# Linear attention and routed experts on one core: fp32 products in halves of the array, and exponentials after the transposes

## The chip, the cores and the metric

The kernel runs on one core of one Trainium2 chip. The metric is the device time of one execution in microseconds (us), the median of three runs. TensorE multiplies matrices, VectorE and ScalarE work on elements and rows, GpSimd does both and issues indirect DMAs, SyncE issues DMAs. Every engine serves its own instructions in order.

## The reference

```python
def phi(x):                                   # x: (4, 8, 576, 64), scaled by 64 ** -0.25
    proj = np.einsum('bhsd,md->bhsm', x, omega)     # 128 features
    h = proj - np.sum(x * x, axis=-1, keepdims=True) / 2.0
    h = h - np.max(h, axis=-1, keepdims=True)
    return np.exp(h) / np.sqrt(m)
q_p, k_p = phi(q_s), phi(k_s)
kv, z = np.einsum('bhsm,bhsd->bhmd', k_p, v), np.sum(k_p, axis=2)
num = np.einsum('bhsm,bhmd->bhsd', q_p, kv)
den = np.einsum('bhsm,bhm->bhs', q_p, z)[..., None] + 1e-06
x = (num / den)                               # as 2304 tokens of 8 * 64 columns
expert_idx = np.argmax(x @ w_gate, axis=1)    # 8 experts
...
h = np.maximum(np.einsum('ecd,edf->ecf', disp, w1), 0.0)   # 512 -> 1024
y = np.einsum('ecf,efd->ecd', h, w2)                       # 1024 -> 512
out[i] = gate_w[i] * y[expert_idx[i], pos[i]]              # up to a capacity per expert
```

## The kernel before, in words

There are three stages, written in one order for every engine.

**Keys.** A pair of heads has nine tiles of 128 tokens; two pairs are handled side by side, one on partitions 0 to 63 and one on 64 to 127, and such a double pair is a chunk (4 batches, 2 chunks each, 72 steps). Keys come transposed, head dimension on partitions. A step projects one tile of both pairs to 256 columns (`project`, L120): the keys are split into two parts of 12 bits (`split`, L113; GpSimd, for the first chunk ScalarE and VectorE), and three products of 256 columns in the rounded 4-byte type add to fp32 accuracy (L122 to L124). `exponent` (L127) takes the maxima of both halves (VectorE, L129) and two exponentials of 128 columns with the maximum as bias (ScalarE, L132). Three steps later `kv_acc` (L188) sums exponentials against values in fp32 (L192: exponentials are the stationary side, 65 columns of values and ones move). After a chunk `kv_gate` (L201) multiplies its sums by the gate weights.

**Queries.** The loop over 18 token tiles has four steps each, one per head pair: projection and exponentials as for the keys, three steps later transposes by TensorE (L446) and a copy to SBUF (ScalarE, L448), six steps later the numerators (`numer`, L451; L462: 73 columns hold sums, denominator and gate logits). `normalise` (L473) divides on VectorE and stores the tile to DRAM. A tile that crosses from one batch to the next has its numerators in two parts of 64 tokens. `route` (L338) turns logits of five to seven tiles into slots and scatters them into a table (GpSimd, L92); `first_item` (L396) and `first_rows` (L427) read the first token's expert, load and split its weights, load a table's rows (L312), gather tokens (GpSimd, L317) and transpose them (`transpose_x`, L324). These are generators: the loop calls `steps` twice per step, and each call advances every one to its next `yield`; `pause(n)` waits n calls.

**Items.** An item is 576 slots of one expert; three run here, the others are skipped by a condition. `mm1` (L649) is the first product, 8 x 2 banks of 12 products (L656 to L658) with evictions on ScalarE and VectorE (L661 to L666); `mm2` and `mm2_rest` (L668, L680) are the second, the last 64 slots in two column halves side by side (L685, fp32). During an item weights and rows of the next are loaded, split (`HI_AT`, `LO_AT`; high parts on GpSimd, L108, low parts mostly on VectorE, L111) and transposed. The remaining routing runs in the first product of the first item (`il`, L717).

PSUM has eight banks of 512 columns: three for projections and first products, two for sums, numerators and second products, two for transposes, one for small things.

Of the kernel before, what the change touches and what calls it, by code (L numbers as in the profile page):

```python
# [24 lines left out]
SLOTS = 576              # slots of one expert item  # L25
FIRST_CUTS = [0, 128, 384, 768, 1152]  # the first keys come in parts
# [5 lines left out]
T0 = 5                   # token tiles that the first item looks at  # L32
QT = 3                   # most token tiles of a query chunk
# [7 lines left out]
HI_AT = ({0: ((1, 2), (1, 3), (2, 0), (2, 1), (2, 2), (2, 3))}, {0: ((2, 0),), 1: ((2, 1),), 3: ((2, 2),), 4: ((2, 3),)})  # L41
LO_AT = ({0: ((1, 2),), 1: ((1, 3),), 3: ((2, 0),), 4: ((2, 1),)}, {1: ((2, 0),), 2: ((2, 1),), 5: ((2, 2),), 6: ((2, 3),)})
# [8 lines left out]
def attention_moe(ctx, tc, kT, qT, va, om, wg, w1, w2, cap, ident, tri, desc, lst, tab0, out):  # L51
# [7 lines left out]
    ps = ctx.enter_context(tc.tile_pool(name="ps", bufs=2, space=PSUM))  # L59
# [4 lines left out]
    def bank(tag, name, bufs=2):  # L64
        return ps.tile([128, 512], F32, tag=tag, name=name, bufs=bufs)

    om_sb = const.tile([128, M], F32, name="om_sb")
    whi = const.tile([128, 2 * M], F32R, name="whi")
    wlo = const.tile([128, 2 * M], F32R, name="wlo")
# [4 lines left out]
    # counts of tokens: small whole numbers, exact in bfloat16  # L74
# [14 lines left out]
    # Slots are unique, so are the tokens behind them: scatters into one array  # L89
    # touch different rows and need no order among themselves.  # L90
# [13 lines left out]
    def split_hi(hi, raw, eng=None):  # L104
        if eng is nc.scalar:
            nc.scalar.copy(hi, raw)
        else:
            nc.gpsimd.tensor_scalar(hi, raw, 1.0, 1.0, op0=ALU.mult, op1=ALU.mult)  # L108

    def split_lo(lo, raw, hi, eng=None):  # L110
        (eng or nc.gpsimd).tensor_tensor(lo, raw, hi.bitcast(F32), op=ALU.subtract)  # L111

    def split(hi, lo, raw, ehi=None, elo=None):  # L113
        split_hi(hi, raw, ehi)
        split_lo(lo, raw, hi, elo)
# [4 lines left out]
    def project(hi, lo, nm, spare=False):  # L120
        pj = (bank("tr", f"pj{nm}") if spare else bank("pj", f"pj{nm}", 3))[:, 0 : 2 * M]
        nc.tensor.matmul(pj, hi, whi, start=True, stop=False)  # L122
        nc.tensor.matmul(pj, lo, whi, start=False, stop=False)  # L123
        nc.tensor.matmul(pj, hi, wlo, start=False, stop=True)  # L124
        return pj

    def exponent(pj, nm):  # L127
        mx = small.tile([128, 2], F32, tag="mx", name=f"mx{nm}", bufs=6)
        nc.vector.tensor_reduce(mx, pj.rearrange("p (a m) -> p a m", a=2), op=ALU.max, axis=AX.X, negate=True)  # L129
        ex = small.tile([128, 2 * M], F32, tag="ex", name=f"ex{nm}", bufs=6)  # L130
        for i in range(2):
            nc.scalar.activation(  # L132
                ex[:, i * M : (i + 1) * M], pj[:, i * M : (i + 1) * M], AF.Exp, bias=mx[:, i : i + 1], scale=1.0
            )
        return ex

# [5 lines left out]
    def load_q(c):  # L142
        n0, n1 = QB[c] * 128, QB[c + 1] * 128
        w = n1 - n0
        raw = qp.tile([128, NP, QT * 128], F32, tag="qraw", name=f"qraw{c}")
        nc.sync.dma_start(raw[:, :, 0:w], qT[:, :, n0:n1])
        qc[c] = raw, w

    def split_q(c, p):
        if p == 0:  # L150
            hi = qp.tile([128, NP, QT * 128], F32R, tag="qhi", name=f"qhi{c}")
            lo = qp.tile([128, NP, QT * 128], F32R, tag="qlo", name=f"qlo{c}")
            qc[c] = hi, lo, *qc[c]
        hi, lo, raw, w = qc[c]
        split(hi[:, p, 0:w], lo[:, p, 0:w], raw[:, p, 0:w])

# [4 lines left out]
    kp = kstack.enter_context(tc.tile_pool(name="kpool", bufs=2))  # L161
    chunks, first = {}, []

    def load_k(b, g):
        raw = kp.tile([128, W], F32, tag="kraw", name=f"kraw{b}{g}")
        hi = kp.tile([128, W], F32R, tag="khi", name=f"khi{b}{g}")
        lo = kp.tile([128, W], F32R, tag="klo", name=f"klo{b}{g}")
        v = kp.tile([128, 2, 10 * VW], F32, tag="v", name=f"v{b}{g}")
        src = va[b, :, 2 * g : 2 * g + 2, :]
        if b == 0 and g == 0:  # L170
            for i, (c0, c1) in enumerate(zip(FIRST_CUTS, FIRST_CUTS[1:])):
                nc.sync.dma_start(raw[:, c0:c1], kT[b, :, g * W + c0 : g * W + c1])
                if i == 2:
                    nc.sync.dma_start(v[:, :, 0 : 4 * VW], src[:, :, 0 : 4 * VW])
# [6 lines left out]
        chunks[b, g] = hi, lo, v, raw  # L181

    def split_k(b, g, c0, c1, ehi=None, elo=None):
        hi, lo, _, raw = chunks[b, g]
        split(hi[:, c0:c1], lo[:, c0:c1], raw[:, c0:c1], ehi, elo)

    # a pair's 9 token tiles: 4 of head A, one of both, 4 of head B
    def kv_acc(b, g, t, ex, acc):  # L188
        v = chunks[b, g][2]
        a, z, o = (t, t + 1, 0) if t < 4 else ((4, 6, 0) if t == 4 else (t + 1, t + 2, VW))  # L190
        for i in range(2):
            nc.tensor.matmul(  # L192
                acc[:, i * 2 * VW + o : i * 2 * VW + o + (z - a) * VW],
                ex[:, i * M : (i + 1) * M],
                v[:, i, a * VW : z * VW],
                start=(t == 0 and i == 0),
                stop=(t == 8),
                skip_group_check=True,
            )

    def kv_gate(b, g, acc):  # L201
        yield from pause(2)
        kv = kv_sb[b][:, 4 * g : 4 * g + 4, :]
        nc.vector.tensor_copy(kv[:, :, 0:VW], acc[:, 0 : 4 * VW].rearrange("p (h c) -> p h c", h=4))
        yield from pause(2 if (b, g) < (B - 1, 1) else 16)
        kvc = small.tile([128, 2 * M], F32, tag="kvc", name=f"kvc{b}{g}", bufs=1)
        nc.scalar.copy(kvc.rearrange("p (h c) -> p h c", h=4), kv[:, :, 0:D])
        yield from pause(4)
        tr = bank("tr", f"ktr{b}{g}")
# [5 lines left out]
        yield from pause(4)  # L215
        sm = bank("sm", f"ksm{b}{g}", 1)
        for i in range(2):
            nc.tensor.matmul(
                sm[:, i * 2 * E : (i + 1) * 2 * E],
                kvT[:, i * M : (i + 1) * M],  # L220
                wg_sb[:, 2 * g + i, :],
                start=True,
                stop=True,
            )
# [5 lines left out]
    # the tensor engine's clock rises with use: keep it busy until the first keys are there  # L230
# [594 lines left out]
```

## Time and profile before

| | us |
|---|---|
| median of 3 runs | 338.39 |
| lowest, highest | 337.31, 339.58 |
| span of the profiled execution | 336.1 |
| keys, until the last sums | 71.0 |
| queries | 85.1 |
| three items | 169.8 |
| after the last transposes | 10.1 |

The profiled execution has no other time than its span, from the first to the last instruction. The stages are read from the trace: the last key sums end at 71.0, the first product of the first item starts at 156.1.

### The profile page before, as it was taken

The page shows a single profiled execution, that of the slowest core. Times are in us where ns is not written, and L with a number is a line of the kernel's source. Part 1 is how long each engine was busy: PE and PEld are TensorE (multiplying, and loading weights), DVE is VectorE, ACT ScalarE, POOL GpSimd, SP SyncE. Part 2 cuts the span into 40 slices and gives each one's busy share as a digit, 9 for nine tenths or more (in the row PEclk, how much of TensorE's full clock was granted, in tenths as well). Part 3 has the DMA queues.
Part 4 walks back from the last instruction along what each step waited for, and adds up shares of the span by engine and source line. Part 5 has one row for each costly group of instructions (what it writes and reads, how often), then busy time and mean ns, then how long its engine had stood idle before and what let it go on. Part 6 is the DMA issues. An engine that isn't in the chain of part 4 may idle for free.

```text
span 336.1 us, 6517 instructions
## 1 busy us (share of the span) xinstructions
PE 311.6 (93%) x2237; PEld 284.5 (85%) x2237; DVE 190.7 (57%) x499; ACT 154.1 (46%) x484; POOL 159.8 (48%) x181
## 2 busy tenths in 40 slices
PE   8999999999999993999399999999999999999960
PEld 6899999999998993899399688899968899968850
DVE  5566556668789984787978133333544525336320
ACT  4677777788886884584112211322322122222120
POOL 2563553886056746638807285167023338304220
PEclk9799999999999999899879999999999999999995
DMA  7446789941954239412000595067062119226010
GB/s 212 178 155 201 249 270 368 352 126 37 288 180 157 66 69 373 171 65 95 0 2 2 155 357 209 33 184 241 0 204 94 62 39 317 69 66 234 33 54 20
DMA packets 30817, 50.34 MB, mean 150 GB/s; under 512 B 5571, under 2 KB 18243, under 8 KB 30756
## 3 DMA queue, kind: packets, MB, share of 16 engines
q1 hardware_dynamic: 27476, 41.46, 37.9%
q0 software_dynamic: 3152, 8.28, 7.2%
q8 instruction: 20, 0.33, 0.5%
q14 instruction: 25, 0.20, 0.3%
q10 hardware_dynamic: 144, 0.07, 0.1%
HBM read 36.80 MB, written 13.28 MB: 149 GB/s over the span
## 4 chain that ended last, share of the span: by engine, by line
PE 79%; DMA 7%; DVE 5%; issue 3%; POOL 2%; SPq 1%; ACT 1%; POOLq 0%; ACTq 0%; DVEq 0%
PE kacc L192 8%; PE hi L656 8%; PE hi L658 7%; PE hi L657 7%; PE yi L673 6%; PE yi L674 6%; PE yi L675 6%; PE qacc L462 6%; PE pjk L122 3%; PE qtr L446 3%; PE xtri L329 3%; PE pjq L122 3%; PE pjk L123 2%; PE pjk L124 2%; DVE dr L351 2%
## 5 line engine op out<-in xcount | busy, mean ns | idle before, releaser
L656 PE MATMUL hi<-xhi,w1hi 128*128 128x288 f32 x192 | 57.8, 301 | 5.1 <-DVE hloi L664 5.1
L658 PE MATMUL hi<-xlo,w1hi 128*128 128x288 f32 x192 | 57.3, 298 | 0.0
L657 PE MATMUL hi<-xhi,w1lo 128*128 128x288 f32 x192 | 57.3, 298 | 0.0
L132 ACT ACTIVATE ex<-pjk,mx 128x128 f32<-128x128 f32 x144 | 44.8, 366 | 18.7 <-DVE mx L129 17.7
L92 POOL DMA_INDIRECT out<-ysi,idx x15 | 17.4, 1161 | 71.6 <-ACT ysi L703 56.1
L132 ACT ACTIVATE ex<-pjq,mx 128x128 f32<-128x128 f32 x144 | 45.9, 377 | 9.2 <-DVE mx L129 9.0
L661 ACT ACTIVATE hhii<-hi 128x288 fp32r<-128x288 f32 (+1 forms) x48 | 18.3, 384 | 56.3 <-PE hi L658 50.6
L192 PE MATMUL kacc<-v,ex 128*128 128x65 f32 (+1 forms) x288 | 41.5, 267 | 1.2 <-DMA v<-va 0.8
L656 PEld LDWEIGHTS hi<-xhi,w1hi 128*128 128x128 f32 x192 | 36.8, 192 | 5.5 <-DVE hloi L664 5.4
L129 DVE TENSOR_REDUCE mx<-pjk 128x2 f32<-128x256 f32 x72 | 30.3, 424 | 19.0 <-PE pjk L124 17.7
L664 DVE SCALAR_TENSOR_TENSOR hloi<-hi,hhii 128x288 fp32r<-128x288 f32 (+1 forms) x48 | 20.4, 424 | 36.2 <-ACT hfi L663 23.5
L462 PE MATMUL qacc<-kv_sb,qpT 128*128 128x73 f32 (+1 forms) x320 | 40.0, 262 | 0.7 <-DVE xr L485 0.7
L192 PEld LDWEIGHTS kacc<-v,ex 128*128 128x128 f32 x288 | 39.1, 194 | 1.6 <-ACT ex L132 1.6
L673 PE MATMUL yi<-w2hi,hhii 128*128 128x512 f32 x96 | 38.9, 405 | 0.0
L462 PEld LDWEIGHTS qacc<-kv_sb,qpT 128*128 128x128 f32 (+1 forms) x320 | 36.2, 182 | 2.5 <-issue 1.3
L674 PE MATMUL yi<-w2hi,hloi 128*128 128x512 f32 x96 | 37.9, 395 | 0.0
L675 PE MATMUL yi<-w2lo,hhii 128*128 128x512 f32 x96 | 37.9, 395 | 0.0
L657 PEld LDWEIGHTS hi<-xhi,w1lo 128*128 128x128 f32 x192 | 36.7, 191 | 0.0
L129 DVE TENSOR_REDUCE mx<-pjq 128x2 f32<-128x256 f32 x72 | 30.1, 418 | 11.8 <-PE pjq L124 8.2
L658 PEld LDWEIGHTS hi<-xlo,w1hi 128*128 128x128 f32 x192 | 36.7, 191 | 0.0
L335 DVE TENSOR_TENSOR xlo<-xtri,xhi 128x512 fp32r<-128x512 f32 (+1 forms) x20 | 12.6, 637 | 38.3 <-ACT xhi L333 38.3
L703 ACT ACTIVATE ysi<-yi,idx 128x512 f32<-128x512 f32 x12 | 8.3, 688 | 54.5 <-issue 45.9
(123 smaller groups left out, 687.5 us busy)
## 6 DMA issues: line engine op xcount, KB each, us to landing
w1raw<-w SPq DMA_DIRECT2D x16, 512.0 KB, 6.0
w2raw<-w SPq DMA_DIRECT2D x16, 512.0 KB, 6.1
out<-zero_sb SPq DMA_DIRECT2D x6, 768.0 KB, 7.0
qraw<-qT SPq DMA_DIRECT2D x6, 768.0 KB, 5.2
x_d<-xr SPq DMA_DIRECT2D x18, 256.0 KB, 2.4
v<-va SPq DMA_DIRECT2D x7, 650.0 KB, 5.0
kraw<-kT SPq DMA_DIRECT2D x7, 576.0 KB, 6.5
v<-va SPq DMA_DIRECT2D x1, 390.0 KB, 7.1
```

Source lines behind the costliest of these rows:

```text
L122: nc.tensor.matmul(pj, hi, whi, start=True, stop=False)
L129: nc.vector.tensor_reduce(mx, pj.rearrange("p (a m) -> p a m", a=2), op=ALU.max, axis=AX.X, negate=True)
L132: nc.scalar.activation(ex[:, i * M : (i + 1) * M], pj[:, i * M : (i + 1) * M], AF.Exp, bias=mx[:, i : i + 1], scale=1.0)
L192: nc.tensor.matmul(acc[:, i * 2 * VW + o : i * 2 * VW + o + (z - a) * VW], ex[:, i * M : (i + 1) * M], v[:, i, a * VW : z * VW], start=(t ...
L462: nc.tensor.matmul(acc[r0:r1, o : o + ROW], qpT[:, i * M + r0 : i * M + r1], kv_sb[b][:, h, :], start=(h % 4 == 0), stop=(h % 4 == 3), ski ...
L656: nc.tensor.matmul(pt, whi_[:, k, fs], xhi[:, k, sl], start=(k == 0), stop=False)
L657: nc.tensor.matmul(pt, wlo_[:, k, fs], xhi[:, k, sl], start=False, stop=False)
L658: nc.tensor.matmul(pt, whi_[:, k, fs], xlo[:, k, sl], start=False, stop=(k == 3))
L664: nc.vector.scalar_tensor_tensor(hlo[:, f, sl], pt[:, 0:w], 0.0, hhi[:, f, sl].bitcast(F32), op0=ALU.max, op1=ALU.subtract)
L673: nc.tensor.matmul(pt, hhi[:, f, sl], w2hi, start=(f == 0), stop=False)
L674: nc.tensor.matmul(pt, hlo[:, f, sl], w2hi, start=False, stop=False)
L675: nc.tensor.matmul(pt, hhi[:, f, sl], w2lo, start=False, stop=(f == 7))
```

## The change

- **Projections** are fp32 products without splits. Omega stands once on each half of the partitions; each head pair uses its 64 rows, and writes its own bank. The two halves of a unit are issued one after the other.
- **Groups.** Four steps' projections are issued together (eight units), into two banks per group; two groups of banks alternate. Sums follow two groups later.
- **Sums, numerators and the gate products** are issued as two products with 64 columns of the stationary side each, to partitions 0 to 63 and 64 to 127.
- **Exponentials of the keys.** The first bank keeps four of 128 columns with the maximum as bias; for the second VectorE adds the maxima and ScalarE takes one of 512 columns.
- **Queries.** A token tile is one step. The shifted projections are transposed, then exponentials of 512 columns write the transposed tile to SBUF. The shift of the first bank is ScalarE's copy and GpSimd's addition, of the second four of ScalarE's with bias. One pair of banks holds a tile's eight numerators, normalised at once.
- **Loads.** Four key chunks are requested at the start. The zeros for the output are written in the first product of the first item instead of in the key stage.
- **Splits.** High parts of weights are ScalarE's (the first two chunks of the first item remain GpSimd's), low parts VectorE's; in the first item they are spread over the steps of the first product.
- **Generators** advance once per `run`, ten times per query tile, and can wait for a place in TensorE's order (`yield "T"`, `"N"`). Pauses are shorter where steps are longer. Rows of `w1` are reordered on the host to fit the new order of heads.

```diff
+    def project(parts, banks):
+        for k, x in enumerate(parts):
+            for i in range(2):
+                rows = slice(64 * i, 64 * i + 64)
+                nc.tensor.matmul(banks[i][:, k * M : (k + 1) * M], x[rows, :], om_s[rows, :], start=True, stop=True)
...
         for i in range(2):
+            for f in (0, 64):
+                nc.tensor.matmul(
+                    acc[f : f + 64, i * 2 * VW + o : i * 2 * VW + o + (z - a) * VW],
+                    ex[:, 4 * i + k, f : f + 64],
+                    v[:, i, a * VW : z * VW],
...
+    for n in range(NK + NT + 3):
+        kn, t = n, n - NK
         if n < NK:
+            pj = [bank(2 * (n % 2) + i, f"pjk{n}{i}") for i in range(2)]
+            project([chunks[b, g][0][:, u * 128 : (u + 1) * 128] for b, g, u in KU[KG * n : KG * n + KG]], pj)
+        elif t < NT:
+            pj = [bank((2 * t + i) % 3, f"pjq{n}{i}") for i in range(2)]
...
+            project([qc[c][:, p, o : o + 128] for p in range(NP)], pj)
+        run("T")
+        if 0 <= t - 1 < NT:
+            d = d_l.pop(t - 1)
+            trs = [bank(3 + i, f"qtr{n}{i}") for i in range(2)]
+            for u in range(H):
+                nc.tensor.transpose(trs[u // 4][:, (u % 4) * M : (u % 4 + 1) * M], d[:, u, :], id_sb)
+        run()
+        if 0 <= n - 2 < NK:
...
+                kv_acc(b, g, u, ex, k, acc_l[0])
...
+        elif 0 <= t - 2 < NT:
+            acc_l[0] = pair(f"qacc{t}")
+            numer(t - 2, qT_l.pop(t - 2), acc_l[0])
+        run("N")
+        if n < NK:
+            ex = kp.tile([128, H, M], F32, tag="ex", name=f"ex{n}", bufs=3)
+            maxima(mx, 0, units(pj[0]))
+            run()
+            for k in range(4):
+                nc.scalar.activation(ex[:, k, :], pj[0][:, k * M : (k + 1) * M], AF.Exp, bias=mx[:, k : k + 1], scale=1.0)
+            maxima(mx, 1, units(pj[1]))
+            run()
+            nc.vector.tensor_tensor(ex[:, 4:8, :], units(pj[1]), spread(mx, 1), op=ALU.add)
+            nc.scalar.activation(ex[:, 4:8, :], ex[:, 4:8, :], AF.Exp)
...
+            if t < NT:
+                d = qp.tile([128, H, M], F32, tag="d", name=f"d{t}", bufs=2)
+                nc.scalar.copy(d[:, 0:4, :], units(pj[0]))
+                maxima(mx, 1, units(pj[1]))
+                run()
+                maxima(mx, 0, d[:, 0:4, :])
+                nc.gpsimd.tensor_tensor(d[:, 0:4, :], d[:, 0:4, :], spread(mx, 0), op=ALU.add)
...
+            if 0 <= t - 1 < NT:
+                qpT = qp.tile([128, H, M], F32, tag="qpT", name=f"qpT{t}", bufs=2)
+                for i in range(2):
+                    nc.scalar.activation(qpT[:, 4 * i : 4 * i + 4, :], units(trs[i]), AF.Exp)
...
+            if t < NT:
+                for k in range(4):
+                    nc.scalar.activation(
+                        d[:, 4 + k, :], pj[1][:, k * M : (k + 1) * M], AF.Identity, bias=mx[:, 4 + k : 5 + k], scale=1.0
+                    )
+                run()
+            if 0 <= t - 2 < NT:
+                normalise(t - 2, acc_l[0])
...
+            run(times=3)
...
                 for i, c in HI_AT[j > 0].get(f, ()):
                     split_w_hi(i, c)
-                if j == 0 and f == 0:
-                    for c in (2, 3):
-                        split_w_lo(2, c, nc.gpsimd)
+                if j == 0 and f < 6:
+                    zero_out(3 * f)
```

## Rows read from the trace of the kernel before

**Rows 1.** Busy time by stage: us, each engine's busy us (x instructions), clock, DMA share.
```profile
10.00:70.90 60.90, 60.13 (x517) 60.12 (x516) 37.53 (x97) 43.88 (x143) 35.18 (x49) 0.97 0.71 241
71.00:156.10 85.10, 79.00 (x702) 75.98 (x701) 67.71 (x251) 64.66 (x221) 48.77 (x59) 0.98 0.46 151
156.10:189.06 32.96, 27.83 (x197) 27.30 (x196) 24.78 (x67) 6.50 (x23) 17.15 (x14) 0.90 0.07 19
...
217.40:243.05 25.65, 25.65 (x195) 25.49 (x194) 11.36 (x20) 7.28 (x24) 12.52 (x11) 1.00 0.44 139
```

**Rows 2.** Timeline, TensorE, one key step: start us, us, engine, line, operation.
```profile
41.12 0.37 PE L122 MATMUL pjk<-whi,khi 128*128 128x256 f32 x1
...
41.56 0.56 PE L192 MATMUL kacc<-v,ex 128*128 128x65 f32 x4
41.92 0.36 PE L122 MATMUL pjk<-whi,khi 128*128 128x256 f32 x1
```

**Rows 3.** Costliest groups, keys: busy us, mean ns | idle before, releaser.
```profile
L132 ACT ACTIVATE ex<-pjk,mx 128x128 f32<-128x128 f32 x128 | 40.2, 365 | 14.6 <-DVE mx L129 13.6
...
L129 DVE TENSOR_REDUCE mx<-pjk 128x2 f32<-128x256 f32 x64 | 27.2, 425 | 18.9 <-PE pjk L124 17.7 <-ACT ex L132 0.9
```

**Rows 4.** The chain that ended last, in order of time: start us, us, what.
```profile
3.61 7.07 DMA v<-va
...
70.63 0.39 PE kacc L192 x4
```

**Rows 5.** Waits in the queries: who for whom, us in total, times, longest.
```profile
PE xtri L329 <- DMA xg<-x_d,idx: 5.1, 1, 5.1
```

**Rows 6.** Timeline, GpSimd, end of the first scatters and the first gather.
```profile
117.21 0.97 POOL L92 DMA_INDIRECT tab_d<-pay,slot  x1 [0.30 <-issue]
...
118.83 1.00 POOL L111 TENSOR_TENSOR qlo<-qraw,qhi 128x384 fp32r<-128x384 f32 x1
...
127.61 1.07 POOL L317 DMA_INDIRECT xg<-x_d,idx  x1 [6.22 <-DMA idx<-tab_d]
```

**Rows 7.** Timeline, start of the first item, three engines.
```profile
157.97 4.08 POOL L108 TENSOR_SCALAR w2hi<-w2raw 128x1024 fp32r<-128x1024 f32 x4
...
159.17 7.57 DVE L351 TENSOR_TENSOR dr<-lg,mxr 128x48 f32<-128x48 f32 x1
...
167.85 0.61 PE L656 MATMUL hi<-xhi,w1hi 128*128 128x288 f32 x1 [5.13 <-DVE hloi L664]
```

**Rows 8.** Timeline, TensorE, query steps: two whole, two of a crossing tile.
```profile
87.65 0.36 PE L122 MATMUL pjq<-whi,qhi 128*128 128x256 f32 x1
...
88.68 0.37 PE L122 MATMUL pjq<-whi,qhi 128*128 128x256 f32 x1
...
90.45 0.48 PE L462 MATMUL qacc<-kv_sb,qpT 128*64 128x73 f32 x8
...
91.63 0.48 PE L462 MATMUL qacc<-kv_sb,qpT 128*64 128x73 f32 x8
```

**Rows 9.** Costliest groups by form, weight loads of the crossing tiles: busy us, mean ns.
```profile
L462 PEld LDWEIGHTS qacc<-kv_sb,qpT 128*64 128x64 f32 x64 | 2.8, 146 | 1.5 <-issue 1.3 <-DVE rec L483 0.2
```

**Rows 10.** The chain that ended last: column halves of the second product.
```profile
243.08 3.58 PE yi1r L685 x16
```

**Rows 11.** Timeline, TensorE, transposes from 64 rows between two products.
```profile
216.66 0.40 PE L675 MATMUL yi<-w2lo,hhii 128*128 128x512 f32 x1
216.99 0.46 PE L329 MATMUL xtri<-id_sb,xg 64*128 64x64 f32 x4
...
217.62 0.30 PE L657 MATMUL hi<-xhi,w1lo 128*128 128x288 f32 x1
```

**Rows 12.** Costliest groups by form, VectorE.
```profile
L485 DVE TENSOR_TENSOR xr<-qacc,rec 128x292 f32<-128x292 f32 x36 | 16.2, 451 | 2.1 <-DMA x_d<-xr 2.0
...
L335 DVE TENSOR_TENSOR xlo<-xtri,xhi 128x512 fp32r<-128x512 f32 x16 | 10.9, 690 | 26.8 <-ACT xhi L333 26.8
```

**Rows 13.** Costliest groups by form, ScalarE.
```profile
L703 ACT ACTIVATE ysi<-yi,idx 128x512 f32<-128x512 f32 x12 | 8.3, 688 | 54.5 <-issue 45.9 <-PE yi L675 8.6
```

More of the change, by code (lines that the diff above doesn't have):

```diff
@@ L32 @@
 T0 = 5
+KB = 4
 QT = 3
@@ L120, in project @@
[L120 to L135, printed above, removed]
+        (eng or nc.vector).tensor_tensor(lo, raw, hi.bitcast(F32), op=ALU.subtract)
@@ new lines, in attention_moe, with start, run @@
+    tasks = []
+    def start(gen):
+        tasks.append([gen, None])
+    def run(at=None, times=1):
+        for _ in range(times):
+            for task in list(tasks):
+                if task[1] is None or task[1] == at:
+                    try:
+                        task[1] = next(task[0])
+                    except StopIteration:
+                        tasks.remove(task)
+    def project(parts, banks):
[3 more added lines that the diff above has]
+                nc.tensor.matmul(banks[i][:, k * M : (k + 1) * M], x[rows, :], om_s[rows, :], start=True, stop=True)
@@ L138, in attention_moe, with units, maxima, spread @@
+    def units(x):
+        return x.rearrange("p (a m) -> p a m", m=M)
+    def maxima(mx, i, src):
+        nc.vector.tensor_reduce(mx[:, 4 * i : 4 * i + 4], src, op=ALU.max, axis=AX.X, negate=True)
+    def spread(mx, i):
+        return mx[:, 4 * i : 4 * i + 4].unsqueeze(2).to_broadcast([128, 4, M])
     qstack = ExitStack()
@@ L229, in attention_moe @@
     load_k(0, 0)
[L231 removed]
+    warm = const.tile([128, 256], F32, name="warm")
     nc.vector.memset(warm, 0.0)
[L233 to L235 removed]
+    wps = bank(SM, "wps")
     for _ in range(WARM):
@@ L438, in first_rows @@
             held.append(i)
[L439 removed]
+            yield "T"
+            yield from transpose_x(i, "i0", SM)
             held.pop()
             yield from pause(3)
[L443 to L449 removed]
@@ L471, in attention_moe, with numer @@
-    xrows = {}
-    def normalise(t, half, acc):
-        yield from pause(1)
-        if half == 0:
-            xrows[t] = small.tile([128, ROW, H], F32, tag="xr", name=f"xr{t}", bufs=3)
-        xr = xrows[t]
-        av = acc[:, 0 : 4 * ROW].rearrange("p (h c) -> p c h", c=ROW)
-        den = small.tile([128, 4], F32, tag="den", name=f"den{t}{half}")
-        nc.vector.tensor_scalar(den, av[:, D, :], EPS, None, op0=ALU.add)
-        yield
-        rec = small.tile([128, 4], F32, tag="rec", name=f"rec{t}{half}")
+    def numer(t, qpT, acc):
+        for p in range(NP):
+            for i in range(2):
+                for r in (0, 64):
+                    nc.tensor.matmul(
+                        acc[r : r + 64, i * 512 + p * ROW : i * 512 + (p + 1) * ROW],
+                        qpT[:, 4 * i + p, r : r + 64],
+                        kv_sb[(t * 128 + r) // S][:, 2 * p + i, :],
+                        start=(p == 0),
+                        stop=(p == NP - 1),
+                        skip_group_check=True,
+                    )
@@ L497, in attention_moe @@
-    QU = [(t, p) for t in range(NT) for p in range(NP)]
-    NK, NQ = len(KU), len(QU)
-    LA, LB = 3, 6
-    ex_l, qT_l, acc_l, tasks = {}, {}, {}, [first_splits()]
-    def steps(gens):
-        return [x for x in gens if next(x, 0) is None]
-    for n in range(NK + NQ + LB + 2):
-        pj = None
-        if n < NK:
-            b, g, t = KU[n]
-            hi, lo = (x[:, t * 128 : (t + 1) * 128] for x in chunks[b, g][0:2])
-            pj = project(hi, lo, f"k{n}", n % 4 == 3 and n < NK - 4)
-        elif n < NK + NQ:
-            t, p = QU[n - NK]
+            xr.rearrange("p c (i h) -> p c i h", i=2),
```

282 lines of the change are left out of this document (105 added, 177 removed).

## The prediction

> **What bounds the kernel now.** I read the table by stage first, then one step of each stage in order of time, then the waits of the stages that lose time. The table [rows 1] is to show that TensorE fills every stage: it is busy for 60.1 of the 60.9 us of the keys, 79.0 of 85.1 us of the queries, and 25.65 of 25.65 us in the first product of the second item. Two stages lose something: the queries 6.1 us, and the first product of the first item, which takes 32.96 us where the same work takes 25.65 in the second.
>
> One step of the keys [rows 2] takes 0.80 us, 41.12 to 41.92: 0.44 for the three projection products, 0.36 for the sums. It yields 256 exponentials in each row. VectorE and ScalarE each wait in it [rows 3]: VectorE 17.7 us for the projection, ScalarE 13.6 us for the maxima. So the keys go by TensorE, and the last sums start at 70.63 [rows 4].
>
> In the queries 5.1 us of the lost time are one wait of the transposes for gathered rows [rows 5], and GpSimd, whose gather fills them, had itself stood 6.22 us for the index load [rows 6]. In the first item a small VectorE operation takes 7.57 us, beside GpSimd's unbroken splits; products then wait 5.13 us and start at 0.44 us in place of 0.30 [rows 7], at a granted clock of 0.90 in that stage [rows 1].
>
> **Part 1, products in halves.** Every fp32 product is two instructions: the x4 in [rows 2] are two products. What a half costs is shown by the one query tile that crosses from one batch to the next: its numerators already come in 64-column halves. Its step is 1.18 us (90.45 to 91.63) against 1.03 (87.65 to 88.68) [rows 8]. The halves aren't slow: sixty-four weight loads of 146 ns, 9.3 us in sum, keep the loader busy for 2.8 [rows 9], so three lie side by side, and sixteen half products of 512 columns take 3.58 us [rows 10], 0.45 a pair, which is 512 columns passed twice at 2.4 GHz with both halves side by side. For 73 columns that makes 0.061 a pair, four pairs 0.245. They replace four instructions of 0.09 (0.36 for four [rows 2]) to 0.11, and the step still grew by 0.15: two changes of the array's shape cost 0.27 to 0.35; I take 0.18 each. Row halves show about the same: from the product at 216.66 to that at 217.62 lie 0.96 us [rows 11], of which 512 columns, four times 64 passed twice and 288 are work, 0.21 + 0.21 + 0.12 at 2.4 GHz; 0.4 is left for two changes with all gaps.
>
> What no row shows is two row halves side by side: the transposes in [rows 11] use one half alone. From below: a pair takes what 128 columns passed twice need, 0.11 us, so a unit's two pairs 0.22. From above: one after another, 0.44, as much as now. I take 0.22, since column halves do overlap [rows 9, 10], and keep 0.44 as a rival.
>
> A group of four key tiles (eight units) then costs TensorE 8 x 0.11 for projections, 16 x 0.058 for sums and two changes: 0.88 + 0.93 + 0.36 = 2.17 us. The gate logits of each key chunk add two transposes, one more change and four pairs, 0.64 per chunk, which is 0.28 per group: 2.45, where four steps now take 3.2 and the logits come on top.
>
> The Trainium skill ("TensorE: Matmul & The Clock Gate", section The mechanism) says that weight loads overlap a running product only where their row groups differ. By that rule the row halves would overlap and the column halves would not; the loads of [rows 9] overlap in the same row group, so here the trace disagrees. By the rule alone the sums of a key group would need 1.9 us in place of 0.93, and the time would be some 25 us above my forecast; I count it with the last rival below.
>
> **Part 2, wider VectorE and ScalarE work for the keys.** A group has two maxima of 512 columns and one addition of 512: 256 columns take 0.425 [rows 3], 512 take 0.69 [rows 12], so 3 x 0.69 = 2.07; the copies for the logits stay, about 1.04 per chunk (two of 256 columns at 0.425, one small), 0.46 per group: 2.53. ScalarE has four exponentials of 128 columns at 0.314 (40.2 us for 128 [rows 3]) and one of 512 at 0.69 [rows 13], with its copy 2.15. So VectorE becomes the bound of the keys, with TensorE 0.1 behind. I take 2.65 a group, since both have to alternate; 2.5 to 3.0 are the ends. The start doesn't move: the rest of the first values lands at 10.7 (3.61 + 7.07 [rows 4]), and with four chunks requested at once it won't come earlier. Two of 18 groups are past their exponentials by 10: 10 + 16 x 2.65 = 52.4, and 2 for the last sums: keys end at 54.5 in place of 71.0, **-16.5**; the ends are 52 and 60.
>
> **Part 3, queries.** A tile costs TensorE 0.88 for projections, 8 x 0.11 for transposes (two fill what projection and numerators leave of 1.03 [rows 2, 8]), 16 x 0.061 for numerators, three changes: 3.3, against 4.1 for four steps now. ScalarE: a copy and two exponentials of 512 columns, four shifts of 128: 3 x 0.69 + 1.26 = 3.3. VectorE: two maxima at 0.69, a normalisation of 584 columns at 0.76 (292 take 0.45 [rows 12]) and three small steps, 2.7. GpSimd: one addition of 512, 1.34 by 384 columns in 1.0 [rows 6]. Four engines near 3.3 in one ring: 3.5 a tile. Sixteen full tiles and 5 us of filling and emptying: 61.
>
> Then what comes on top. GpSimd's old work, the splits, was due a chunk later; the new addition is due in the next tile, and it stands behind the gathers. From the end of the last scatter of the first tiles (118.18) to the first gather lie 9.4 us [rows 6]; with two gathers of 1.1 the addition comes 8.7 us late beyond the tile that it has. TensorE can run only one projection meanwhile. Twelve scatters at 1.0 delay it too, some 4.5 in all. The routing's small steps on VectorE, now in a ring without slack, 6; five transposes of gathered rows with ScalarE's copies, 3. Sum 22, and 61 + 22 = 83 against 85.1: **-2**. Ends: 70 (the wait for the index lies beside other work, routing is hidden) and 90.
>
> **Part 4, the items.** Splitting of the first item's weights leaves GpSimd, so VectorE's small operation no longer waits, and the first product should take what it takes in the second item: 32.96 - 25.65, **-7.3** (ends 0 and 8). The six splits go to ScalarE, 1.1 us each by 128 and 512 columns [rows 3, 13], which was busy 6.5 of 33 us [rows 1]; three product banks, each filled in 1.6 us (25.65 for sixteen), cover each. Two low parts go to VectorE, which was busy 24.8 us, 7.6 of them waiting: they fit, narrowly; without that room the gain is 2.5 smaller. Zeroing of the output, six DMAs of SyncE, moves from the keys into a stage with a DMA share of 0.07 [rows 1]; behind it on SyncE stand the index and weights of the second item, needed a whole product later, so I price it at nothing, at most 2.
>
> **Sum.** 336.1 - 16.5 - 2 - 7.3 = 310.3 us of span. The median of the runs lies 2.3 above the profiled span of 336.1; with that, **312 us**.
>
> **Rivals.** *GpSimd's wait is covered*: the index lands within the tile, the ring isn't held, minus 8.7 and 2 of slow clock: 301. For it: DMA is busy for only 0.46 of that stage [rows 1], so index and scatter may land sooner; against: 9.4 us is nearly three tiles. *Row halves don't overlap*: TensorE needs 3.33 a key group (16 x 0.68 = 11 more) and 4.15 a tile (10 more, 4 of it beside waits): 329. For it: no row shows them together. *The ring of the queries doesn't close in 3.5 us* (the slower side): projection, copy, maximum, GpSimd's addition, transposes, two exponentials and numerators are 7.2 us in a row, over six hand-overs between engines that serve in order. If a tile takes 5.6, that is 17 x 2.1 = 36 more: 348. It decides from 5.05 us a tile, (338 - 312) / 17 above 3.5. For it: a hand-over already stops TensorE here, which waits for a gather that waited for an index [rows 5, 6]; against: the work is spread over three tiles. *The change doesn't do what it says*, halves run one after another in both directions: 4.4 a key group, 5.2 a tile less 12 of covered waits: 29 + 15 more, 356. Against it: [rows 9, 10].
>
> **How the numbers follow.** Forecast 0.54 (its own range 303 to 322), covered wait 0.16, row halves apart 0.15, ring 0.08, halves apart 0.07. A measurement of this kernel can tell about 1% from no change: 335.0 and 341.8. Faster: 0.54 + 0.16 + 0.12 of the row-half case, 0.82. Same: 0.03 of that case, 0.02 of the ring, 0.01 of the last, 0.06. Slower: 0.12. The range reaches from the covered wait with a shorter key stage (297) to the row halves apart with a little more (332); beyond it lie the ring, the last case and the edges of the others, 0.2.
>
> **What would show it.** Right: two projections of a unit starting together, key groups 2.6 us apart with VectorE over 90% busy, last key sums near 54; a wait of GpSimd for the index with TensorE idle beside it; a first product of 26 us in the first item. Wrong: pairs of projections 0.2 us apart; tiles at 5 us without routing beside them; no gap at the gathers.

## The result, and the profile after

The changed kernel takes 326.95 us (326.74 to 330.25) against 338.76 for the kernel before beside it: ratio 0.970, interval 0.964 to 0.976. The forecast was 312. It is faster, but by 11.8 us in place of 26. The profiled execution took 327.09, its span is 325.3. Ratios here and below compare runs in the same state, so they differ a little from the ratios of the medians.

The table by stage of the changed kernel: keys, queries, first product of the first item, first product of the second.

```profile
core 0: us, PE busy (x) PEld busy (x) DVE busy (x) ACT busy (x) POOL busy (x), PEclk, DMA share, GB/s
10.00:63.40 53.40, 45.58 (x936) 40.38 (x932) 38.48 (x74) 32.39 (x94) 1.04 (x1) 1.00 0.52 186
63.40:150.45 87.05, 68.33 (x1009) 59.45 (x1005) 57.26 (x162) 49.38 (x128) 36.96 (x36) 0.91 0.45 151
150.45:177.46 27.01, 26.63 (x199) 26.09 (x199) 20.03 (x68) 12.25 (x29) 6.46 (x7) 0.98 0.58 199
205.80:231.45 25.65, 25.65 (x195) 25.49 (x196) 11.36 (x20) 11.02 (x28) 6.52 (x6) 1.00 0.44 140
```

Set beside [rows 1]: TensorE's work in the keys fell from 60.1 to 45.6 us, but the stage has 7.8 us in which TensorE does nothing, where it had 0.8. The keys end at 63.4 (71.0 before, 54.5 forecast), the queries last 87.1 (85.1 before, 83 forecast), the first product 27.0 (32.96 before, 25.65 forecast). What follows it takes 147.8 in place of 147.0. The four misses, 8.9 + 4.1 + 1.3 + 0.8, are the 15 us between the forecast's 310.3 and the span.

Where the keys wait is seen in one group with a gate, in order of time (the columns are those of [rows 2]):

```profile
15.49 0.43 DVE L211 COPY kv_sb<-kacc 128x260 f32<-128x260 f32 x1 [0.69 <-PE kacc L200]
15.84 1.28 DVE L153 TENSOR_REDUCE mx<-pjk 128x4 f32<-128x512 f32 x2
16.07 1.16 PE L147 MATMUL pjk<-om_s,kraw 64*128 64x128 f32 x16
16.64 1.14 ACT L512 ACTIVATE ex<-pjk,mx 128x128 f32<-128x128 f32 x4 [1.17 <-DVE mx L153]
...
17.65 0.42 ACT L214 COPY kvc<-kv_sb 128x256 f32<-128x256 f32 x1
...
18.13 0.44 PE L220 MATMUL ktr<-id_sb,kvc 128*128 128x128 f32 x2 [0.89 <-ACT kvc L214]
18.49 1.36 PE L200 MATMUL kacc<-v,ex 128*64 128x65 f32 x32
...
19.79 1.16 PE L147 MATMUL pjk<-om_s,kraw 64*128 64x128 f32 x16
...
22.15 1.16 PE L147 MATMUL pjk<-om_s,kraw 64*128 64x128 f32 x16
```

This group takes 3.72 us (16.07 to 19.79), the next, without transposes for the gate, 2.36; of the last fourteen groups the six with such transposes take 3.7 to 4.0, the others 2.2 to 2.6. Read it backwards: the transposes for the gate logits (18.13) wait for ScalarE's copy (17.65), which stands behind four exponentials (16.64), which wait for the maxima; and the maxima (15.84) stand behind VectorE's copy of the sums (15.49), which waits for the sums themselves. The transposes are queued right behind a projection, so the sums of the next group stand still too. The waits of the stage, with sum, times and longest:

```profile
ACT ex L512 <- DVE mx L153: 16.2, 15, 1.5
PEld ktr L220 <- ACT kvc L214: 8.7, 7, 1.6
DVE kv_sb L211 <- PE kacc L200: 8.0, 8, 3.4
PE ktr L220 <- ACT kvc L214: 7.4, 7, 1.4
```

TensorE's 7.4 us are nearly all of the 7.8. The end of the stage holds a second delay, from the last exponentials (58.40) to the last sums (63.36):

```profile
57.74 0.66 ACT L516 ACTIVATE ex<-ex 128x512 f32<-128x512 f32 x1
...
59.58 1.16 PE L147 MATMUL pjq<-om_s,qraw 64*128 64x128 f32 x16
...
61.19 1.09 PE L491 MATMUL qtr<-id_sb,d 128*128 128x128 f32 x8 [0.44 <-POOL d L526]
62.21 1.15 PE L200 MATMUL kacc<-v,ex 128*64 128x65 f32 x32
```

The last sums stand in TensorE's order behind the second query tile's projections and the first one's transposes. In the queries an undisturbed tile takes 3.3 to 3.5 us (forecast 3.5; the first two lines below); the ring stops where the additions stand behind indirect DMAs:

```profile
77.53 1.25 PE L441 MATMUL qacc<-kv_sb,qpT 128*64 128x73 f32 x32
...
80.83 1.25 PE L441 MATMUL qacc<-kv_sb,qpT 128*64 128x73 f32 x32
...
96.73 1.09 PE L491 MATMUL qtr<-id_sb,d 128*128 128x128 f32 x8 [1.18 <-POOL d L526]
96.86 1.18 POOL L100 DMA_INDIRECT tab_d<-pay,slot  x1 [0.18 <-issue]
...
97.76 1.25 PE L441 MATMUL qacc<-kv_sb,qpT 128*64 128x73 f32 x32
...
102.20 0.97 POOL L100 DMA_INDIRECT tab_d<-pay,slot  x1 [0.30 <-issue]
102.67 0.17 DVE L455 TENSOR_SCALAR den<-qacc 128x8 f32<-128x8 f32 x1 [4.33 <-remote]
...
103.19 1.05 POOL L526 TENSOR_TENSOR d<-d,mx 128x512 f32<-128x512 f32 x1
...
104.30 1.97 PE L491 MATMUL qtr<-id_sb,d 128*128 128x128 f32 x8 [3.54 <-POOL d L526]
...
109.12 0.99 POOL L310 DMA_INDIRECT xg<-x_d,idx  x1 [4.88 <-DMA idx<-tab_d]
```

Five scatters hold an addition until 103.19, TensorE idles 3.54 us, and its next eight transposes take 1.97 in place of 1.09. The clock row of the four us behind this wait shows why, 0.50, the lower of its two levels (1.2 in place of 2.4 GHz):

```profile
104.30:108.30 4.00, 4.00 (x40) 3.56 (x40) 1.30 (x2) 2.82 (x7) 0.00 (x0) 0.50 0.18 43
```

The gather then waits 4.88 for its index, as [rows 6] showed for the kernel before.

### The profile page after: what moved, and what is told of

Read it like the earlier page. It is cut to its first block, busy times and chain, and to the rows that moved or that the text cites. A ratio compares the mean times of both kernels' runs of the same rounds, so it can differ in the third digit from the quotient of the medians.

```text
span 325.3 us, 7425 instructions
## 1 busy us (share of the span) xinstructions
PE 283.7 (87%) x2957; PEld 244.8 (75%) x2957; DVE 168.3 (52%) x383; ACT 150.9 (46%) x364; POOL 78.2 (24%) x80
## 4 chain that ended last, share of the span: by engine, by line
PE 63%; DVE 10%; issue 7%; DMA 5%; POOL 5%; ACT 4%; SPq 1%; another core or an unknown queue 1%; POOLq 0%; ACTq 0%; DVEq 0%
PE hi L654 8%; PE hi L652 8%; PE hi L653 7%; PE yi L669 6%; PE yi L670 6%; PE yi L671 6%; PE kacc L200 5%; DVE mx L153 4%; PE pjk L147 3%; PE qacc L441 3%; PE qtr L491 3%; POOL d L526 2%; ACT ex L512 2%; PE xtri L322 2%; DMA kraw<-kT 2%
## 5 line engine op out<-in xcount | busy, mean ns | idle before, releaser
L526 POOL TENSOR_TENSOR d<-d,mx 128x512 f32<-128x512 f32 x18 | 19.1, 1062 | 96.5 <-DVE mx L153 92.5
L100 POOL DMA_INDIRECT out<-ysi,idx x15 | 15.3, 1022 | 91.3 <-ACT ysi L699 75.3
L491 PE MATMUL qtr<-id_sb,d 128*128 128x128 f32 x144 | 22.3, 303 | 11.9 <-POOL d L526 11.8
L512 ACT ACTIVATE ex<-pjk,mx 128x128 f32<-128x128 f32 x72 | 20.6, 368 | 20.3 <-DVE mx L153 20.3
L441 PE MATMUL qacc<-kv_sb,qpT 128*64 128x73 f32 x576 | 26.1, 249 | 4.2 <-issue 3.4
L441 PEld LDWEIGHTS qacc<-kv_sb,qpT 128*64 128x64 f32 x576 | 23.2, 154 | 7.9 <-issue 4.2
L310 POOL DMA_INDIRECT xg<-x_d,idx x20 | 22.7, 1133 | 26.6 <-issue 10.1
L491 PEld LDWEIGHTS qtr<-id_sb,d 128*128 128x128 f32 x144 | 17.7, 154 | 14.7 <-POOL d L526 13.9
L153 DVE TENSOR_REDUCE mx<-pjk 128x4 f32<-128x512 f32 x36 | 23.0, 682 | 3.8 <-PE pjk L147 3.8
```

The costliest lines, as they stand in the source:

```text
L153: nc.vector.tensor_reduce(mx[:, 4 * i : 4 * i + 4], src, op=ALU.max, axis=AX.X, negate=True)
L310: nc.gpsimd.indirect_dma_start(out=big["xg"][0:n, i, :], out_offset=None, in_=x_d[0:rows, :], in_offset=bass.IndirectOffsetOnAxis(ap=big[" ...
L441: nc.tensor.matmul(acc[r : r + 64, i * 512 + p * ROW : i * 512 + (p + 1) * ROW], qpT[:, 4 * i + p, r : r + 64], kv_sb[(t * 128 + r) // S][ ...
L491: nc.tensor.transpose(trs[u // 4][:, (u % 4) * M : (u % 4 + 1) * M], d[:, u, :], id_sb)
L512: nc.scalar.activation(ex[:, k, :], pj[0][:, k * M : (k + 1) * M], AF.Exp, bias=mx[:, k : k + 1], scale=1.0)
L526: nc.gpsimd.tensor_tensor(d[:, 0:4, :], d[:, 0:4, :], spread(mx, 0), op=ALU.add)
```

## The experiments

All times in one table: median, ratio to the kernel before on the same chip with its interval, end of the keys, and length of the queries to the first product of the items. The groups e1 to e4, e5 to e8, e9 to e12, e13 to e15 and e16 to e18 ran on five chips; the chip of the first profiles isn't on record. In the profiles of e2, e8 and e11 the keys began partly at the lower clock (granted clock 0.80, 0.82 and 0.50 from 12 to 18 us, 1.00 in all others); this delays their keys by some 2, 2 and 5 us.

| | us | ratio | keys end | queries |
|---|---|---|---|---|
| e1 gate later | 312.7 | 0.929 (0.920 to 0.939) | 55.1 | 81.3 |
| e2 gathers later | 317.5 | 0.939 (0.930 to 0.949) | 65.5 | 78.6 |
| e3 full numerators | 328.3 | 0.972 (0.958 to 0.987) | 62.7 | 86.3 |
| e4 additions on VectorE | 319.7 | 0.949 (0.940 to 0.958) | 63.8 | 79.6 |
| e5 unaltered | 326.6 | 0.970 (0.965 to 0.975) | 62.5 | 86.2 |
| e6 splits on GpSimd | 332.8 | 0.988 (0.983 to 0.992) | 63.2 | 87.1 |
| e7 e1 and e2 | 315.4 | 0.935 (0.930 to 0.941) | 55.4 | 82.6 |
| e8 e7, three additions on VectorE | 313.9 | 0.923 (0.918 to 0.927) | 57.7 | 81.6 |
| e9 e1 again | 318.0 | 0.942 (0.937 to 0.947) | 55.9 | 85.2 |
| e10 spread scatters | 314.3 | 309.3 to 316.1 us | 55.6 | 80.5 |
| e11 full sums | 334.3 | 330.4 to 340.1 us | 71.6 | 84.7 |
| e12 rows in turn | 331.5 | 0.983 (0.979 to 0.986) | 66.6 | 86.8 |
| e13 e1, full numerators | 317.3 | 0.946 (0.938 to 0.954) | 55.3 | 84.5 |
| e14 e10, scatters behind the queries | 312.0 | 0.926 (0.920 to 0.933) | 55.9 | 74.4 |
| e16 e14, scatters at once | 304.2 | 0.907 (0.901 to 0.912) | 55.7 | 71.6 |
| e18 unaltered, one run | 325.1 | | 63.4 | 84.3 |

**The gate (e1, e9).**

```diff
     def kv_gate(b, g, acc):
+        yield from pause(2 if (b, g) < (B - 1, 1) else 6)
         kv = kv_sb[b][:, 4 * g : 4 * g + 4, :]
```

> The sums of a key chunk are copied two generator steps later (behind the maxima of the group instead of ahead of them), so that the transposes for the gate logits come one group later. Theory (the gate's waits in order set 3.7 to 4.0 us of a group in place of 2.3 every second or third time): groups with a gate shrink to about 2.6 us, the last key sums end near 56 in place of 63.3, and the time is 319 to 321. Rival (the gate's own work is what fills those groups, TensorE and VectorE both busy): groups stay near 3.7, the time stays within 2 us of 327.

> The first variant (gate copies later) unaltered, beside the next three. Theory (its gain is the gate's waits, whatever the chip): 311 to 314, keys end at 55. Rival (a part of the 14 us was an execution without late numerators): with late numerators in its profile it takes 315 to 318.

The keys end at 55.1 and 55.9. By the ratios the kernel gains 4.1 points on one chip and 2.8 on the other, each against the changed kernel's 0.970 on other chips. In e1 that is twice what I expected: the keys give 8.3 us, but the queries are 5.8 shorter too and the first product 1.1, beside the first profile of the changed kernel. In e9 it is 9.4 us of 337, and beside late numerators (below) 318 was the rival's time. The stage of e9, on the same rows:

```profile
10.00:55.90 45.90, 45.56 (x930) 40.80 (x926) 38.87 (x76) 34.11 (x99) 1.84 (x2) 1.00 0.59 215
```

TensorE has the same work as in the changed kernel, 45.56 against 45.58 us, in 7.5 us less. The waits of the transposes for the copy are gone, and the copy of the sums now stands behind a maximum:

```profile
15.09 1.29 DVE L153 TENSOR_REDUCE mx<-pjk 128x4 f32<-128x512 f32 x2 [0.30 <-PE pjk L147]
...
16.07 1.16 PE L147 MATMUL pjk<-om_s,kraw 64*128 64x128 f32 x16
16.30 0.42 DVE L212 COPY kv_sb<-kacc 128x260 f32<-128x260 f32 x1
...
18.46 1.16 PE L147 MATMUL pjk<-om_s,kraw 64*128 64x128 f32 x16
...
19.55 0.44 PE L221 MATMUL ktr<-id_sb,kvc 128*128 128x128 f32 x2
...
50.38 0.63 ACT L517 ACTIVATE ex<-ex 128x512 f32<-128x512 f32 x1 [0.30 <-DVE ex L516]
...
54.72 1.15 PE L200 MATMUL kacc<-v,ex 128*64 128x65 f32 x32
```

The last fourteen groups now take 2.17 to 2.75 us, 2.5 in the mean. The last sums still end 4.9 us behind the last exponentials (the last two lines).

**GpSimd in the queries (e2, e4).** e2 sets `pause(20)` in place of `pause(6)` ahead of the gathers in `first_rows`; e4 has

```diff
-nc.gpsimd.tensor_tensor(d[:, 0:4, :], ...
+(nc.vector if t > 5 else nc.gpsimd).tensor_tensor(d[:, 0:4, :], ...
```

> The gathers of the first item's rows are placed 14 generator steps (about one and a half query tiles) later, behind the load of their index. Theory (GpSimd stands 4.9 us for the index with the additions of the query tiles queued behind it): GpSimd's wait falls under 1 us, the queries are 3 to 6 us shorter, 321 to 324. Rival (the wait is only passed on, since the ring of the tiles is held by the scatters and late numerators just as long): GpSimd's wait goes, the time stays within 1.5 us of 327. Second rival (the gathered rows are now late at the first item): the first product starts later than 150.5.

> From the seventh token tile on VectorE makes the addition of the first bank instead of GpSimd. Theory (scatters, gathers and the index wait hold the additions, and these the transposes): the transposes' waits for GpSimd, 11.4 us in sum, go; VectorE has about 0.6 us more per tile on 2.8 and stays under the 3.4 of TensorE: queries 5 to 8 us shorter, 319 to 322. Rival (VectorE with the routing's small steps becomes the bound, or late numerators set the pace): waits for VectorE take their place, within 2 us of 327.

The query stage of e2, and the wait that is new in e4:

```profile
65.50:144.05 78.55, 63.53 (x1008) 55.70 (x1005) 56.68 (x163) 48.65 (x127) 35.91 (x35) 0.96 0.51 168
```

```profile
118.56 1.12 PE L322 MATMUL xtri<-id_sb,xg 128*128 128x128 f32 x4 [6.62 <-DMA xg<-x_d,idx]
```

Both shorten the queries, by 5.7 and 4.7 us against the 84.3 of e18 (one profile each, e18 on another chip): either the wait for the index is taken out of GpSimd's queue, or the additions are. In e2 the transposes still wait 10.6 us for additions (13.1 in e18), mostly behind the scatters; the rest of its gain is TensorE's busy time, 63.5 us in place of 66.1, with fewer products at the lower clock. e2 gained more than expected, e4 in time what was expected. In e4 a new wait stands at the end, TensorE 6.6 us for gathered rows, since the tiles no longer wait for GpSimd but the gathers still wait for the index.

**Both, and the additions behind scatters (e7, e8).** e8 gives VectorE the additions of tiles 10, 11 and 14.

> Later gate copies (as in the first variant) and later gathers (as in the second) together. Theory (the gate's waits and GpSimd's wait for the index are separate): keys end at 55, GpSimd's wait for the index is under 1 us, the time is 308 to 310. Rival (what the later gathers gained came from late numerators, which the later gate copies end too): the index wait goes but the time stays within 1.5 us of the 312.7 of the first variant.

> As the variant with both, and for three tiles, the ones whose addition stands behind scatters or gathers, VectorE makes the addition. Theory (the additions behind the indirect DMAs are the last of GpSimd's waits): the transposes' waits for GpSimd fall from 9 us to under 3, products behind them run at full clock, 303 to 306. Rival (VectorE, which carries the routing in the same tiles, becomes late): waits for VectorE instead, within 2 us of the variant with both.

e7 is 0.035 below e5 on the same chip, 11.7 us: beside the gate's 9.4 of e9 (another chip) that leaves some 2 for the gathers, where e2 alone lay 3.1 points, 10 us, below 0.970 on a chip without late numerators. How much of this is the chip was not tested. e8's ratio is 0.012 lower than e7's, but its six runs spread from 311.1 to 316.3 us and its median lies 1.5 us below e7's, so this gain is hardly shown. They end 5 and 8 us above the upper ends of their theories; in both, numerators were late.

**Splits of the first item back on GpSimd (e6).** `HI_AT` and `LO_AT` of the kernel before for the first item, high parts and two low ones on GpSimd.

> The changed kernel with the first item's six high parts and two low parts on GpSimd again, issued at the first step as in the kernel before. Theory (moving them is all that shortened the first product): a small VectorE operation of 6 to 8 us beside the splits returns, the first product of the first item takes 32 to 33 us in place of 27, the time is 5 to 7 us above the changed kernel run beside it. Rival (the fuller pipeline or the earlier clock is what shortened it): the first product stays under 29, the time within 2 us.

It is 6.1 us above e5, its first product 32.24 us against 27.26 there. The VectorE operation of [rows 7] is back:

```profile
L344 DVE TENSOR_TENSOR dr<-lg,mxr 128x48 f32<-128x48 f32 x1 | 6.0, 6012 | 0.0
```

**Halves of the array (e3, e11, e12, e13).** e3 and e13 make the numerators of a tile inside one batch products of 128 columns, e11 the key sums; e12 swaps the two loops of `project`.

> Numerators of tiles that lie in one batch are products of 128 columns, as in the kernel before; only crossing tiles keep two halves. Theory (numerators in column halves, issued while GpSimd issues its indirect DMAs, end 2 to 4 us late; those of 128 columns do not): the four late groups, 3.9, 3.8, 2.3 and 1.9 us, go, the undisturbed tile stays at 3.4 to 3.5 us, the queries are 5 to 10 us shorter, 317 to 322. Rival (any product in that place would be late): four groups stay late, the time stays within 2 us of 327.

> The variant with later gate copies, with numerators of 128 columns where a tile lies in one batch. Theory (any signal of TensorE can come late beside GpSimd's indirect DMAs, whatever the product's shape, and some chips show it and others not): late numerators here too on a chip that shows them, none on one that does not; undisturbed tiles at 3.85 us in place of 3.4, the time 1 to 5 us above the same variant with halves. Rival (only column halves are late): no late group on a chip on which the kernel before shows any, and the time is 2 to 5 us below.

> The first variant with the key sums as products of 128 columns instead of two halves side by side. Theory (a pair of halves takes 0.058 us and a full product 0.18, less one change of shape of 0.17): a key group's TensorE work grows by 0.3 us, keys end 4 to 6 us later, 316 to 319. Rival (VectorE sets the key groups, TensorE has room): groups stay at 2.5 us, within 1 us of the first variant.

> The first variant with the projections of one row half issued first and then those of the other, so that neighbours use the same rows. Theory (two row halves overlap only where neighbouring products use different rows): sixteen products take 1.9 to 2.0 us in place of 1.1, key groups 3.2 in place of 2.5 and tiles 4.2 in place of 3.4: 335 to 342. Rival (products overlap far apart in the queue too, or the group has room): within 3 us of the first variant.

Key sums of e11, projections of e12, and numerators of two query tiles of e13, the second of which lies in two batches and keeps its halves (each from its kernel's order of time):

```profile
32.91 1.90 PE L200 MATMUL kacc<-v,ex 128*128 128x65 f32 x16
```

```profile
35.02 1.71 PE L147 MATMUL pjk<-om_s,kraw 64*128 64x128 f32 x16
```

```profile
69.71 1.90 PE L444 MATMUL qacc<-kv_sb,qpT 128*128 128x73 f32 x16
...
73.66 1.25 PE L444 MATMUL qacc<-kv_sb,qpT 128*64 128x73 f32 x32
```

Full products take 1.90 us for what thirty-two half instructions do in 1.15 (sums; 1.36 where a product of 130 columns is among them) or 1.25 (numerators). In e11 the keys end 15.7 us later than in e9. About 5 of these lie at the start, where TensorE's clock was lower in e11's profile:

```profile
10.00:15.00 5.00, 5.00 (x36) 4.76 (x38) 1.98 (x3) 2.35 (x6) 0.00 (x0) 0.61 1.03 408
```

From the fifth group on a group takes 3.2 us in place of 2.5, which is the 0.75 between 1.90 and 1.15, and gives 9.6 in thirteen groups. My 4 to 6 was too low, since I priced a full instruction at 0.09 and sixteen take 0.12 each. In e12 rows in turn take 1.71 in place of 1.16, less than the 1.9 that I expected; groups take 3.0, the keys end 10.7 us later, and the time rises by 13.5. Both kinds of halves earn their place. Undisturbed tiles of e13 take 3.85 to 4.2 us, and it is 4.6 us above e1 (another chip, also without late numerators), within its theory. e3 came out as its rival said. On neither chip of e3 and e13 were numerators late in any kernel profiled there, so these two say nothing on their cause; e3 stays with the changed kernel because slower tiles stand against fewer waits, or because nothing was there to gain.

**Scatters (e10, e14, e16).** e10 spreads the scatters by one more step, with `pause(18)` and `pause(5)` around the gathers; e14 has, on top of it, `pause(25 if z == 12 else 2)` ahead of them; e16 spreads only those of the first tiles.

> As the variant with later gate copies and later gathers, but with one more generator step between scatters (three per query tile at most, then fewer), gathers and transposes moved to fit. Theory (a burst of scatters holds the addition of a tile for about 4 us, a spread one only for one scatter): the transposes' longest wait for GpSimd falls under 2 us, 306 to 310. Rival (the same seconds of GpSimd are only spread over more tiles, each a little late): within 2 us of the variant with later gate copies alone.

> As the spread variant, with the seven scatters of the second group of tiles placed 23 generator steps later, behind the last query tiles, in the first product of the first item. Theory (in the spread variant they stand in front of the last tile's addition and beside its numerators; from the last projection to the first product of the items lie 14.5 us): that stretch falls to 10 to 11 us, 306 to 310 on a chip like that of the last group. Rival (they only delay the next item's index and gathers): the first item is longer by the same amount, within 2 us of the spread variant.

> As the variant with the second group's scatters behind the query tiles, but these seven are issued in one go instead of being spread over the first product. Theory (spread there, they pushed back the routing of the third group and with it the next item's index and rows, which gave back 6 us in the second product): the first product starts near 130 as before, the wait of 4.5 us in the first item's second product goes, 305 to 308. Rival (a burst at that place costs the same elsewhere): 311 to 313.

e10's runs lie too far apart for a ratio, but all four are below the four of e9 on the same chip (317.0 to 319.6). In e14 the first product starts 5.8 us earlier than in e10 (whose chip had late numerators), but the time is 312, the rival's. What follows the first product takes 154.5 us in place of 148.2. In the second product of that item TensorE waits 4.53 us for an addition of VectorE; this waits for a copy of ScalarE, which stands behind a split that waited 11.00 us for the next item's weights:

```profile
167.79 1.04 ACT L116 CAST w1hi<-w1raw 128x1024 fp32r<-128x1024 f32 x1 [11.00 <-DMA w1raw<-w]
168.86 0.58 ACT L698 COPY ysi<-yi0r 64x512 f32<-64x512 f32 x1
```

These weights are chosen by the routing of the last tiles, which the program issues behind the spread scatters: its own scatters begin 21.1 us after the first product's start, in e10 13.4 and in e16 12.8. Moved work gave its gain back. e16 keeps the gain, and is the fastest of all, 304.2 us, on a chip without late numerators:

```profile
10.00:55.70 45.70, 45.37 (x928) 40.60 (x924) 38.87 (x77) 34.06 (x98) 1.78 (x2) 1.00 0.61 216
55.70:127.34 71.64, 63.02 (x1012) 55.62 (x1010) 55.13 (x161) 47.20 (x124) 33.24 (x33) 0.95 0.58 183
127.34:153.24 25.90, 25.90 (x197) 25.60 (x196) 20.00 (x68) 12.84 (x30) 10.50 (x9) 1.00 0.57 196
```

**Late signals (e5, e15, e17, e18).**

> The changed kernel, unaltered, once more. In its first profile four groups of numerators ended 1.9 to 3.9 us late beside GpSimd's indirect DMAs; in the profiles of the four variants before this one none did. Theory (lateness belongs to this program's placement): late groups again at the same places, 326 to 328. Rival (it belonged to one execution or one chip): no late group, and the queries are 3 to 6 us shorter than 87, 321 to 324.

> The kernel before, profiled beside these. Theory (late signals of TensorE beside indirect DMAs belong to some chips, not to the change): on a chip that shows them here, numerators of the kernel before are late beside its scatters and gathers as well, at little cost, since its ring has slack: 336 to 339. Rival (they come with the change): none late, on a chip on which the two other kernels of this group show them.

> The kernel before, for its profile on whichever chip this is. Theory (some chips show late signals of TensorE beside indirect DMAs, whatever the kernel): late here if and only if the changed kernel beside it is late; 336 to 339 either way. Rival (only the changed kernel is late).

> The changed kernel unaltered, for its profile beside the kernel before. Theory: with late numerators 326 to 328, without them 321 to 324 (the variant with later gate copies was 4 to 5 us faster where none were late). Rival (they cost this kernel nothing, since it waits for GpSimd anyway): 326 to 328 in both cases.

In the changed kernel's first profile VectorE's operation at 102.67 waits 4.33 us for numerators that were issued at 97.76 and end in the profile at 99.01. The ends of products are modelled there, so it can't be told whether the signal was late or the work. In e18, the same program, the same place reads

```profile
97.78 1.25 PE L441 MATMUL qacc<-kv_sb,qpT 128*64 128x73 f32 x32
...
99.08 0.17 DVE L455 TENSOR_SCALAR den<-qacc 128x8 f32<-128x8 f32 x1 [0.71 <-PE qacc L441]
...
104.32 0.90 PE L491 MATMUL qtr<-id_sb,d 128*128 128x128 f32 x3 [4.20 <-POOL d L526]
```

The lateness, 2 to 5 us, shows on the chips of e5 to e8 and e9 to e12, not on those of e1 to e4, e13 to e15 and e16 to e18. The kernel before took 336.7 (e15) and 335.4 (e17) with none. The changed kernel loses perhaps 1 to 2 us by it (326.6 to 327 against the single run of 325.1 on another chip, between the theory's time and the rival's), since TensorE waits for GpSimd's addition anyway (4.20 us here); the variant with the later gate may lose 4, the 1.3 points between e1 and e9. Whether the change brings it stays open: the profiles of e15 and e17 are from chips whose other kernels didn't show it, and the first profile of the kernel before shows none on a chip that isn't on record.

## Why the prediction was wrong, point by point

- **Bound and reading of before: right.** TensorE filled the keys, and its work set what could be saved.
- **Part 1: right.** Halves overlap in both directions, also the row halves that no row of before showed: 1.16 us for sixteen projections, 1.15 for thirty-two sums. In e9 a group without steps of the gate takes 2.17 us (13.90 to 16.07), the forecast's price for TensorE. e11 and e12 show what the halves save. The Trainium skill ("TensorE: Matmul & The Clock Gate", section The mechanism) says that weight loads overlap a running product only where their row groups differ. By that rule column halves would not overlap; thirty-two in 1.15 us, as [rows 9] before, show that they do.
- **Part 2: wrong, and the step that failed.** The step is "keys end at 54.5": the wait that the gate's steps cause was put at nothing, and the last sums were sized too small. *The groups*: "I take 2.65 a group" put the last exponentials at 52.4; they end at 58.4. In "the copies for the logits stay, about 1.04 per chunk ... 0.46 per group" and "0.28 per group" on TensorE I priced the gate by its own durations, as if it could lie anywhere. In the changed kernel its steps stand in the queues of three engines ahead of work of the ring, and TensorE stands still for 7.4 us in seven waits for one copy. e1 and e9 show it: one edit, which leaves TensorE the same work, ends these waits, a group takes 2.5 us, and the keys end 7.5 to 8.3 us earlier. *The last sums*: "2 for the last sums" are 5.0 (58.4 to 63.4), and 4.9 in e9, behind the first query tiles' products. The rows show this; no run moved these sums. So there is luck in it that e9 comes near the forecast (55.9 for 54.5): its groups are shorter than 2.65, its last sums 3 us longer. The bound in e9 was TensorE, 45.56 of 45.9 us busy, with VectorE at 38.87, not the other way round.
- **Part 3: right in kind, 4 short.** The undisturbed tile, the wait for the index and the scatters are there. The transposes' waits for the addition sum to 11.4 us in the stage; I had 8.7 + 4.5. For the index alone 8.7 was too much, since e2 gains 5.7 us without that wait, and a part of this is clock. What the sum left out is what follows a wait: products at half clock, 0.91 mean in the stage. TensorE is busy there for 68.3 us, in e2 at 0.96 for 63.5 with as many products, so this is worth some 5 us. e2 and e4 show that the additions behind GpSimd's queue are the cause of the waits; e18 gives 84.3 where signals were not late. The 6 us for routing and the 3 for gathered rows were not tested by themselves.
- **Part 4: right.** e6 prices it at 6.1 us, forecast 7.3. The first product began at half clock after the waits at the end of the queries (0.98 mean) and took 27.0; in e16, at full clock, 25.9 for a forecast of 25.65. Zeroing cost nothing that shows.
- **Rivals.** Row halves apart and halves apart both ways fell by the trace, though the 329 of the first lies nearest to the measured time. A covered wait for the index did not occur, but e2 made it. The ring closed in 3.4 us.

## What to carry to other kernels

When steps of a pipeline are merged into wider ones, side work that used to fit between them has to be placed anew. Here its price was not its duration but the wait at its place in each engine's queue: list what stands behind it there. Moved work gives its gain back if something later waits for what is queued behind it (e14), so follow it to its next reader. An engine that both computes for a tight ring and issues indirect DMAs can stop the ring for a whole burst, as GpSimd's five scatters did here. The waits also cost clock: price the slower products behind them.

## What the runs showed of the hardware that I had not expected

- A full fp32 instruction of 65 columns takes 0.12 us in a row of sixteen (1.90), two halves side by side 0.07 (thirty-two in 1.15).
- Order matters for row halves: alternating, sixteen instructions take 1.16 us; eight of one half and then eight of the other, 1.71.
- On two of five chips, and in the first profile, VectorE starts 2 to 5 us after the profile's end of numerators that it waits for while GpSimd issues indirect DMAs, on the others not; why was not found.
